# Reordering the first 17 microseconds of a one-core kernel: split x load, earlier weights, transposes in halves, fewer identity matmuls

## The chip, the cores and the metric

The kernel runs on one core of a Trainium2 chip. The metric is the device time of one execution in microseconds (us), lower is better; times are medians of several executions. A change counts as faster or slower only beyond 2%.

Names: PE is TensorE, DVE is VectorE, ACT is ScalarE, POOL is GpSimd, SP is SyncE, which only issues loads here.

## The reference, cut to what matters

```
x = A_x                                    # 1 x 2048 x 1024, bf16
xn = layernorm(x)
out = x + ssm(xn, Lambda, B, C, log_dt, Dskip) + mish(xn @ w1 + b1) @ w2
# ssm: complex diagonal recurrence over 2048 steps, state 1024
# w1: 1024 x 3584, w2: 3584 x 1024
```

Nothing can be multiplied before `x` is normalised and transposed. The first product is `xn @ w1`.

## The kernel before: the parts that matter

The sequence is cut in four blocks of 512 rows, and a block in four x tiles (q = 0 to 3) of 128 rows. Each engine has one queue and works through it in the order written (for ScalarE the profile after the change shows it: two copies with their input ready run only after a mean that waited for its load until 8.85 us); semaphores come from the declared reads and writes. The head, up to the first weight matmuls, is this:

```python
# loads on the SP queue: four x tiles of 256 KB, then weights of 512 KB each
for q in range(NQ):
    load_x(SP, 0, q)
...
for i in range(NRING):
    ring_load()                       # weights for two f tiles
    if i == 3: ...                    # load Dskip

def first_mean_a(q):                  # ACT: sum of a tile, then -sum/D
    aop(activation(sq, xx[q], Identity, accum_out=rc(q, 3)))
    aop(activation(mv[q, 0], rc(q, 3), Copy, scale=-1/D))
def first_var_a(q): ...               # ACT: squares, summed
def first_sums_v / first_var_v ...    # DVE: the same statistics

keep_busy(76)                         # identity matmuls: nothing but PE work
for q in range(2): DVE statistics of tile q
first_sqrt(0); first_mean_a(2); first_sqrt(1); first_var_a(2); first_sqrt(2)   # ACT
first_apply(0)                        # DVE: xn of tile 0
first_transpose(0)                    # PE: 8 transposes into PSUM
keep_busy(4)
first_apply(1)
first_transpose(1)
keep_busy(4)
first_copy(0, VE)                     # DVE: PSUM -> xnT, 8 k slices
first_copy(1, VE, 0, 4)               # DVE: k 0..3
first_copy(1, AC, 4, NK)              # ACT: k 4..7
first_mean_a(3); first_var_a(3); first_sqrt(3)
first_apply(2); first_apply(3)

for f in range(6):                    # 256-wide matmuls: tiles 0 and 1 ("first halves")
    first_half(f, 0)
    if f == 0: transpose the parameters, copy to par
    if f in (2, 3): transpose tile f, copy it (DVE)
...                                   # then first_half(f, 1): tiles 2 and 3 ("second halves")
```

Later the second block's x tiles are loaded from the POOL queue, in the middle of POOL's work on phase tables. VectorE takes their statistics at 45 to 55 us.

```python
for j in range(NJ):
    phases(j)                         # three POOL operations
    if j == 3:
        for q in range(NQ):
            load_x(PO, 1, q)
```

Of the kernel before, what the change touches and what calls it, by code (L numbers as in the profile page):

```python
# [5 lines left out]
ALU = mybir.AluOpType  # L6
# [3 lines left out]
P = 128  # L10
# [146 lines left out]
def build_kernel(nc, A_x, A_Lambda_re, A_Lambda_im, A_B_re, A_B_im, A_C_re, A_C_im,  # L157
                 A_log_dt, A_Dskip, B_w1, B_b1, B_w2, out):
    bf16, f32, i32 = DT.bfloat16, DT.float32, DT.int32
    S, D = A_x.shape[1], A_x.shape[2]  # L160
# [4 lines left out]
    NQ = TB // P  # L165
    NK = D // P
# [8 lines left out]
    PE = Queue(nc, "pe")  # L175
    VE = Queue(nc, "ve")
    AC = Queue(nc, "ac")
    PO = Queue(nc, "po")
    SP = Queue(nc, "sp")

    def sb(name, shape, dtype):
        return nc.alloc_sbuf_tensor(name, shape, dtype)
# [4 lines left out]
    b_ring = [Buf("ring%d" % i) for i in range(NRING)]  # L187
# [16 lines left out]
    b_xnT = [Buf("xnT%d" % q, parts=[Buf("xnT%d_%d" % (q, h)) for h in range(2)]) for q in range(NQ)]  # L204
# [3 lines left out]
    xx = sb("xx", [P, 2, NQ, D], bf16)  # L208
    b_xx = [[Buf("xx%d_%d" % (i, q), parts=[Buf("xx%d_%d_%d" % (i, q, h)) for h in range(2)])
             for q in range(NQ)] for i in range(2)]  # L210
# [7 lines left out]
    NST = 3 * NJ + NF  # L218
    st = sb("st", [NST, P], bf16)
    b_st = Buf("st")  # L220
    ident = sb("ident", [P, P], bf16)
    b_ident = Buf("ident")
    par = sb("par", [P, NST], f32)
    b_par = Buf("par")
    stats = sb("stats", [P, 2, 2, 6], f32)
    b_stats = [Buf("stats%d" % i) for i in range(2)]
# [21 lines left out]
    ps = nc.alloc_psum_tensor("ps", [P, 8, TB], f32)  # L248
    b_ps = [Buf("ps%d" % i) for i in range(8)]

    def ps16(i):
        return ps[:, i, :].bitcast(bf16)
# [23 lines left out]
    vop, aop, pop = VE.op, AC.op, PO.op  # L276
# [7 lines left out]
    def load_x(queue, blk, q):  # L284
        r0 = blk * TB + q * P
        i = blk % 2
        queue.dma(lambda e: e.dma_start(xx[:, i, q, :], A_x[0, r0:r0 + P, :]),  # L287
                  s_xx[i][q] if blk else s_x0[q], writes=[b_xx[i][q]])

    for q in range(NQ):  # L290
        load_x(SP, 0, q)
    for src, r0, n in ((A_log_dt, 2 * NJ, NJ), (A_Lambda_im, NJ, NJ), (A_Lambda_re, 0, NJ),
                       (B_b1, 3 * NJ, NF)):
        AC.dma(lambda e, src=src, r0=r0, n=n: e.dma_start(
# [8 lines left out]
    def ring_load():  # L303
        i = n_loaded[0]
        if i >= len(items):
            return
        n_loaded[0] += 1
        kind, g = items[i]
        s = i % NRING
        if kind == "w1":  # L310
            dst = ring[:, s, :].rearrange("p (k f) -> p k f", k=NK)
            src = B_w1[:, g * 256:(g + 1) * 256].rearrange("(k p) f -> p k f", p=P)
        else:
            dst = ring[:, s, :].rearrange("p (f d) -> p f d", f=2)
            src = B_w2[g * 256:(g + 1) * 256, :].rearrange("(f p) d -> p f d", p=P)
        SP.dma(lambda e: e.dma_start(dst, src), s_ring[s], writes=[b_ring[s]])

    for i in range(NRING):
        ring_load()
        if i == 3:  # L320
            SP.dma(lambda e: e.dma_start(dsk[:], A_Dskip.partition_broadcast(P)), s_dsk, writes=[b_dsk])


# [12 lines left out]
    def rc(q, n):  # L336
        return rs[:, q, n:n + 1]

    def first_sums_v(q, h):
        s = q % 2  # L340
        vop(lambda e: e.bn_stats(stats[:, s, h, :], xx[:, 0, q, h * 512:(h + 1) * 512]),
            reads=[b_xx[0][q]], writes=[b_stats[s]])

    def first_var_v(q):
        s = q % 2
        vop(lambda e: e.bn_aggr(mv[:, q, :], stats[:, s, :, :]), reads=[b_stats[s]], writes=[b_mv[q]])

    def first_mean_a(q):
        aop(lambda e: e.activation(sq[:], xx[:, 0, q, :], AF.Identity, bias=kon[:, 1:2], accum_out=rc(q, 3)),
            reads=[b_xx[0][q], b_kon], writes=[b_sq, b_rs[q]])  # L350
        aop(lambda e: e.activation(mv[:, q, 0:1], rc(q, 3), AF.Copy, scale=-1.0 / D),
            reads=[b_rs[q]], writes=[b_mv[q]])

    def first_var_a(q):
        aop(lambda e: e.activation(sq[:], xx[:, 0, q, :], AF.Square, bias=mv[:, q, 0:1], accum_out=mv[:, q, 1:2]),
            reads=[b_xx[0][q], b_mv[q]], writes=[b_sq, b_mv[q]])

    def first_sqrt(q):
        scale = 1.0 if q < 2 else 1.0 / D
        aop(lambda e: e.activation(rc(q, 1), mv[:, q, 1:2], AF.Sqrt, scale=scale, bias=kon[:, 2:3]),  # L360
            reads=[b_mv[q], b_kon], writes=[b_rs1[q]])

    def first_apply(q):
        y = rc(q, 1)
        vop(lambda e: e.reciprocal(y, y), reads=[b_rs1[q]], writes=[b_rs1[q]])
        vop(lambda e: e.tensor_scalar(xn[:, q, :], xx[:, 0, q, :], mv[:, q, 0:1], y,
                                      op0=ALU.subtract if q < 2 else ALU.add, op1=ALU.mult),
            reads=[b_xx[0][q], b_mv[q], b_rs1[q]], writes=[b_xn[q]])

    def bank_T(q, k):  # L370
        if q == 1 and k >= NK // 2:
            return 5
        return 6 + q % 2

    def first_transpose(q):
        for k in range(NK):
            bank = bank_T(q, k)
            PE.mm(lambda e, k=k, bank=bank: e.transpose(ps16(bank)[:, k * P:(k + 1) * P],  # L378
                                                        xn[:, q, k * P:(k + 1) * P], ident[:]),
                  reads=[b_xn[q], b_ident], writes=[b_ps[bank]],  # L380
                  first=k == 0 or bank != bank_T(q, k - 1), last=k == NK - 1 or bank != bank_T(q, k + 1))

    def first_copy(q, queue, k0=0, k1=NK):
        dst = xnT[:, k0:k1, q * P:(q + 1) * P]
        bank = bank_T(q, k0)
        srcp = ps16(bank).rearrange("p (k t) -> p k t", k=NK)[:, k0:k1, :]
        b_dst = b_xnT[q] if k1 - k0 == NK else b_xnT[q].parts[k0 // 4]
        if queue is AC:
            aop(lambda e: e.copy(dst, srcp), reads=[b_ps[bank]], writes=[b_dst])  # L389
        else:  # L390
            vop(lambda e: e.tensor_copy(dst, srcp), reads=[b_ps[bank]], writes=[b_dst])
# [62 lines left out]

    def keep_busy(n):
        for i in range(n):
            PE.mm(lambda e: e.matmul(ps[:, 4, 0:P], lhsT=ident[:], rhs=ident[:], start=True, stop=True),  # L457
                  reads=[b_ident], writes=[b_ps[4]], first=i == 0, last=i == n - 1)

    keep_busy(76)  # L460
    aop(lambda e: e.activation(rs[:, :, 3], kon[:, 2:3].to_broadcast([P, NQ]), AF.Sqrt), reads=[b_kon], writes=b_rs)
    for q in range(2):
        first_sums_v(q, 0)
        first_sums_v(q, 1)
        first_var_v(q)
    first_sqrt(0)
    first_mean_a(2)
    first_sqrt(1)
    first_var_a(2)
    first_sqrt(2)  # L470
    first_apply(0)
    first_transpose(0)
    keep_busy(4)
    first_apply(1)
    first_transpose(1)
    keep_busy(4)
    first_copy(0, VE)
    first_copy(1, VE, 0, 4)
    first_copy(1, AC, 4, NK)
    first_mean_a(3)  # L480
    first_var_a(3)
    first_sqrt(3)
    first_apply(2)
    first_apply(3)
    NSPLIT = 6

    def first_half(f, half):
        s, fi = f // 2, f % 2
        wt = ring[:, s, :].rearrange("p (k f) -> p k f", k=NK)
        ts = slice(half * 256, half * 256 + 256)  # L490
        for k in range(NK):
            PE.mm(lambda e, k=k: e.matmul(ps[:, f, ts], lhsT=wt[:, k, fi * P:(fi + 1) * P], rhs=xnT[:, k, ts],  # L492
                                          start=k == 0, stop=k == NK - 1),
                  reads=[b_ring[s]] + b_xnT[2 * half:2 * half + 2], writes=[b_ps[f]],
                  first=half == 0 and k == 0, last=half == 1 and k == NK - 1)

    for f in range(NSPLIT):
        first_half(f, 0)
        if f == 0:
            PE.op(lambda e: e.transpose(ps16(5)[:, 0:NST], st[:, :], ident[0:NST, 0:NST]),  # L500
                  reads=[b_st, b_ident], writes=[b_ps[5]])
            vop(lambda e: e.tensor_copy(par[:, :], ps16(5)[:, 0:NST]), reads=[b_ps[5]], writes=[b_par])
        if f in (2, 3):
            q = f
            first_transpose(q)
            first_copy(q, VE)

# [345 lines left out]
```

## Time and profile before

| | before |
|---|---|
| median | 624.05 us (623.83 to 624.13, 3 executions) |
| span of the profiled execution | 622.6 us |
| PE busy | 99% of it |
| first weight matmul | 10.40 us |
| second halves start | 16.77 us |

"Second halves start" is the start of the 49th of the 96 matmuls of 256 columns; from there on PE runs without a wait for 70 us, so this is the time at which the head is over. The page of the kernel before gives the span and, per engine, busy us, share and instructions:

```profile
span 622.6 us, 7430 instructions
...
PE 617.8 (99%) x2981; PEld 289.3 (46%) x2981; DVE 464.5 (75%) x684; ACT 246.7 (40%) x162; POOL 50.2 (8%) x47
```

The waits view of PE, the whole span (who waited for whom: us in total, times, longest):

```profile
PE ps L457 <- POOL kon L328: 1.4, 1, 1.4
PE ps L492 <- ACT xnT L389: 0.5, 1, 0.5
PE ps L715 <- DVE mt L663: 0.3, 1, 0.3
```

PE waits once at the start, once for ScalarE's half copy, and once near 93.7 us for VectorE. As far as waits go, only what PE does before 10.4 us is left to gain on it. The timeline of the head (start, duration, engine, line, operation, out<-in, shape, count, idle time before):

```profile
1.41 7.11 PE L457 MATMUL ps<-ident 128*128 128x128 bf16 x76 [1.41 <-POOL kon L328]
...
6.91 0.55 DVE L366 TENSOR_SCALAR xn<-xx,mv,rs 128x1024 bf16<-128x1024 bf16 x1
...
8.36 0.61 PE L378 MATMUL ps<-ident,xn 128*128 128x128 bf16 x8
...
9.68 0.59 ACT L389 COPY xnT<-ps 128x512 bf16<-128x512 bf16 x1 [0.78 <-PE ps L378]
...
10.16 1.15 ACT L349 ACTIVATE sq<-xx,kon 128x1024 bf16<-128x1024 bf16 x1
...
10.40 1.03 PE L492 MATMUL ps<-xnT,ring 128*128 128x256 bf16 x8 [0.54 <-ACT xnT L389]
```

Read it downward: xn of tile 0 is ready at 7.46 us (6.91 + 0.55), but the identity matmuls (L457) hold PE until 8.36 us, when the transposes (L378) start. ScalarE's half copy (L389) ends at 10.27 us and the weight matmuls (L492) follow. The mean of tile 3 (L349) stands behind that copy. The identity matmuls compute nothing that is used; in this trace the step from one to the next falls from 107 to 56 ns at 7.04 us, and "the clock rises" means this step below.

### The profile page before, as it was taken

How to read it: one execution, taken by the hardware profiler on the slowest of the kernel's cores; microseconds unless marked ns; L12 is line 12 of the kernel's file. 1: busy time of each engine (PE TensorE's matmuls, PEld its weight loads, DVE VectorE, ACT ScalarE, POOL GpSimd, SP SyncE). 2: the span in 40 equal slices, each digit the busy share in tenths (PEclk: the TensorE clock that was granted, in tenths of full speed). 3: DMA queues.
4: the chain of work that ended last, by engine and by line, in shares of the span. 5: the costliest groups of instructions: out<-in, count | busy, mean ns of one | idle time of the engine just before them, and what ended most of it. 6: DMA issues, size and time to landing. Idle time of an engine off the chain costs nothing.

```text
span 622.6 us, 7430 instructions
## 1 busy us (share of the span) xinstructions
PE 617.8 (99%) x2981; PEld 289.3 (46%) x2981; DVE 464.5 (75%) x684; ACT 246.7 (40%) x162; POOL 50.2 (8%) x47
## 2 busy tenths in 40 slices
PE   8999999999999999999999999999999999999998
PEld 8644444444444444444444444444444444444443
DVE  4799999999557599998047759999624856999603
ACT  6679996332069950000008992000000999000000
POOL 1899000000100000000010000000000000000000
DMA  9999976750364400864055420285204541033001
GB/s 265 230 274 272 221 142 187 192 164 1 123 188 161 136 0 18 228 172 125 17 186 148 157 103 0 76 222 158 87 34 136 156 149 68 0 126 111 1 0 68
DMA packets 124188, 79.41 MB, mean 128 GB/s; under 512 B 48890, under 2 KB 106490, under 8 KB 124154
## 3 DMA queue, kind: packets, MB, share of 16 engines
q1 hardware_dynamic: 120656, 71.58, 42.2%
q10 hardware_dynamic: 2538, 4.21, 1.8%
q0 software_dynamic: 960, 3.15, 1.6%
q8 instruction: 24, 0.39, 0.3%
q14 instruction: 10, 0.08, 0.0%
HBM read 63.19 MB, written 4.19 MB: 108 GB/s over the span
## 4 chain that ended last, share of the span: by engine, by line
PE 99%; DVE 0%; ACT 0%; POOL 0%; issue 0%; POOLq 0%
PE ps L715 48%; PE ps L638 29%; PE ps L658 18%; PE ps L492 2%; PE ps L457 1%; DVE mt L663 0%; PE ps L378 0%; DVE xx L752 0%; ACT xnT L389 0%; POOL ident L325 0%; POOL ident L324 0%; PE ps L500 0%; POOL kon L328 0%; POOLq L838 0%
## 5 line engine op out<-in xcount | busy, mean ns | idle before, releaser
L715 PE MATMUL ps<-ring,act 128*128 128x512 bf16 x896 | 194.2, 379 | 0.3 <-DVE mt L663 0.3
L638 PE MATMUL ps<-xnT,ring 128*128 128x512 bf16 x848 | 183.7, 379 | 0.0
L616 ACT ACTIVATE act<-hb 128x3584 bf16<-128x3584 bf16 x16 | 50.9, 3183 | 245.5 <-DVE hb L645 245.0
L715 PEld LDWEIGHTS ps<-ring,act 128*128 128x128 bf16 x896 | 87.6, 98 | 106.3 <-DVE mt L663 0.8
L638 PEld LDWEIGHTS ps<-xnT,ring 128*128 128x128 bf16 x848 | 83.0, 98 | 99.8
L645 DVE TENSOR_SCALAR hb<-ps,par 128x512 bf16<-128x512 f32 x112 | 82.9, 748 | 56.2 <-PE ps L638 54.3
L715 PE MATMUL ps<-CT,hT 128*128 128x512 bf16 x512 | 111.2, 379 | 0.0
L658 PE MATMUL ps<-xnT,BT 128*128 128x512 bf16 x512 | 111.2, 379 | 0.0
L663 DVE TENSOR_TENSOR mt<-ps,tab 128x1024 bf16<-128x1024 f32 x64 | 75.4, 1220 | 13.3 <-PE ps L658 11.7
L715 PEld LDWEIGHTS ps<-CT,hT 128*128 128x128 bf16 x512 | 50.1, 98 | 60.4
L658 PEld LDWEIGHTS ps<-xnT,BT 128*128 128x128 bf16 x512 | 50.1, 98 | 60.4
L752 DVE TENSOR_TENSOR xx<-ps,xx 128x1024 bf16<-128x1024 f32 (+1 forms) x17 | 19.5, 1161 | 70.1 <-PE ps L715 70.0
L681 DVE TENSOR_TENSOR_SCAN hT<-cs,qi,hT 128x512 bf16<-128x512 f32 x48 | 58.9, 1270 | 0.0
L618 ACT ACTIVATE act<-act 128x3584 bf16<-128x3584 bf16 x16 | 51.0, 3191 | 0.2
L617 ACT ACTIVATE act<-act 128x3584 bf16<-128x3584 bf16 x16 | 51.0, 3190 | 0.2
L686 DVE TENSOR_TENSOR mt<-hT,tab 128x1024 bf16<-128x1024 bf16 x64 | 41.4, 689 | 1.1
L623 DVE TENSOR_TENSOR act<-act,hb 128x3584 bf16<-128x3584 bf16 x16 | 32.9, 2059 | 1.3 <-ACT act L618 1.3
L287 POOL DMA_DIRECT2D xx<-in_A_x_dram x12 | 6.7, 558 | 254.0 <-DVE xx L752 250.1
L592 ACT ACTIVATE ct<-CT,cs 128x512 f32<-128x512 bf16 x16 | 11.5, 718 | 28.8 <-DVE CT L594 24.5
L617 ACT ACT_TABLE_LOAD x16 | 20.5, 1283 | 0.3
L618 ACT ACT_TABLE_LOAD x16 | 20.5, 1283 | 0.3
L681 DVE TENSOR_TENSOR_SCAN hT<-cs,hT 128x512 bf16<-128x512 f32 x16 | 18.7, 1209 | 0.0
(78 smaller groups left out, 280.4 us busy)
## 6 DMA issues: line engine op xcount, KB each, us to landing
ring<-in_B_w_dram SPq DMA_DIRECT2D x112, 512.0 KB, 3.7
out_dram<-xx ACTq DMA_DIRECT2D x15, 256.0 KB, 2.0
xx<-in_A_x_dram POOLq DMA_DIRECT2D x12, 256.0 KB, 4.2
xx<-in_A_x_dram SPq DMA_DIRECT2D x4, 256.0 KB, 3.5
dsk<-in_A_Dskip_dram SPq DMA_DIRECT2D x1, 256.0 KB, 6.3
out_dram<-xx ACTq DMA_DIRECT2D x2, 128.0 KB, 1.7
xnT<-xn SPq DMA_TRANSPOSE x12, 4.5
BT<-in_A_B_re_dram SPq DMA_TRANSPOSE x8, 5.7
```

Of the source, the lines that this page charges most:

```text
L616: aop(lambda e: e.activation(a, hs, AF.Exp), reads=[b_hb[g % 2]], writes=[b_act[g]])
L617: aop(lambda e: e.activation(a, a, AF.Ln, bias=1.0), reads=[b_act[g]], writes=[b_act[g]])
L618: aop(lambda e: e.activation(a, a, AF.Tanh), reads=[b_act[g]], writes=[b_act[g]])
L623: vop(lambda e: e.tensor_tensor(a, a, hs, op=ALU.mult), reads=[b_act[g], b_hb[g % 2]], writes=[b_act[g]])
L638: PE.mm(lambda e, k=k: e.matmul(ps[:, bank, :], lhsT=wt[:, k, fi * P:(fi + 1) * P], rhs=xnT[:, k, :], start=k == 0, stop=k == NK - 1), rea ...
L645: vop(lambda e: e.tensor_scalar(hb[:, hs, :], ps[:, bank, :], b1(f), None, op0=ALU.add), reads=[b_ps[bank], b_par], writes=[b_hbf[hs]])
L658: PE.mm(lambda e, j=j, ci=ci, k=k, bank=bank: e.matmul(ps[:, bank + ci, :], lhsT=BT[:, ci, j, k, :], rhs=xnT[:, k, :], start=k == 0, stop= ...
L663: vop(lambda e, s=s, u=u, j=j: e.tensor_tensor(mt[:, s, :, :], u, tab[:, s, j, :].unsqueeze(1).to_broadcast([P, 2, TB]), op=ALU.mult), rea ...
L681: vop(lambda e, ci=ci, init=init: e.tensor_tensor_scan(out=hT[:, ci, j, :], data0=cj("r", j).to_broadcast([P, TB]), data1=hT[:, ci, j, :], ...
L686: vop(lambda e, s=s: e.tensor_tensor(mt[:, s, :, :], hT[:, :, j, :], tab[:, s, j, :].unsqueeze(1).to_broadcast([P, 2, TB]), op=ALU.mult), ...
L715: PE.mm(lambda e: e.matmul(ps[:, u, :], lhsT=lhsT, rhs=rhs, start=st_, stop=last), reads=reads, writes=[b_ps[u]], first=st_, last=last)
L752: vop(lambda e: e.tensor_tensor(xr, src, xr, op=ALU.add), reads=b_src + [b_x], writes=[b_x])
```

## The change

Its intent: start the weight matmuls earlier. The first x tile comes in two loads so that statistics start sooner; the first weights are loaded ahead of tiles 2 and 3; 50 instead of 76 identity matmuls; the transposes of tiles 0 and 1 go to halves of four PSUM banks, so that VectorE and ScalarE copy halves side by side; the parameters' transpose moves out of the matmul stream; tile 2's statistics move from ScalarE to VectorE. Two smaller moves come along: tile 3's transposes stand one f later among the first halves, and the load of Dskip two ring loads later. The diff, cut to its core:

```diff
-    for q in range(NQ):
-        load_x(SP, 0, q)
+    for h in range(2):
+        SP.dma(... xx[:, 0, 0, h*512:(h+1)*512] ...)      # tile 0 in two loads
+    load_x(SP, 0, 1)
@@
     for i in range(NRING):
         ring_load()
-        if i == 3:
+        if i == 0:
+            load_x(SP, 0, 2)
+            load_x(SP, 0, 3)
+        if i == 5:
@@
-        if q == 1 and k >= NK // 2:
-            return 5
+        if q < 2 and k >= NK // 2:
+            return 4 + q
@@
-    keep_busy(76)
+    keep_busy(50)
+    PE.op(... transpose of the parameters into bank 2 ...)
     for q in range(2):
         first_sums_v(q, 0); first_sums_v(q, 1); first_var_v(q)
-    first_sqrt(0)
-    first_mean_a(2)
-    first_sqrt(1)
-    first_var_a(2)
-    first_sqrt(2)
+        first_sqrt(q)
     first_apply(0)
     first_transpose(0)
     keep_busy(4)
     first_apply(1)
     first_transpose(1)
-    keep_busy(4)
-    first_copy(0, VE)
+    first_copy(0, VE, 0, 4)
     first_copy(1, VE, 0, 4)
+    first_mean_a(3)
+    first_copy(0, AC, 4, NK)
     first_copy(1, AC, 4, NK)
-    first_mean_a(3)
     first_var_a(3)
     first_sqrt(3)
+    vop(... copy the parameters to par ...)
+    first_sums_v(2, 0); first_sums_v(2, 1)
+    first_var_v(2)
+    first_sqrt(2)
     first_apply(2)
     first_apply(3)
@@ in the loop over the first halves
-        if f == 0: (transpose and copy of the parameters)
-        if f in (2, 3):
+        if f in (2, 4):
```

The first matmuls (k 0 to 3) now wait only for VectorE's halves, and those with k 4 to 7 only for ScalarE's.

## The prediction

> **What bounds the kernel now.** TensorE: the page has it busy 99% of 622.6 us, and the chain of waits is 99% PE. After 10.4 us the waits view gives it one wait of 0.3 us (near 93.7 us), so only the head can give time. In the timeline the weight matmuls start at 10.40 us and their second halves at about 16.77 us (48 at a 0.109 us pitch before 22.01 us). VectorE has no idle time over 0.15 us from 29.3 to 94 us, but its earlier waits are for PE: a shift of the head moves VectorE too and should reach the end.
>
> **The head before.** 76 identity matmuls run 1.41-8.36 us, at 107 ns each until 7.04 us and 56 ns after. xn of tile 0 is ready at 7.46 us, so they hold the transposes up by 0.9 us. A tile's transposes take 0.45 us, the VectorE copy 0.69 us (0.42 for a half), the ScalarE half copy 0.59 us; that copy (9.68-10.27) releases the matmuls. First weights land at 8.75 us, the fourth x tile at 6.95 us.
>
> **What the change gives.** Half loads start the statistics 0.35 us earlier; xn of tile 0 comes at about 7.1 us. Fifty identity matmuls end at about 6.75 us, so the transposes start at about 7.15 instead of 8.36 us and those of tile 1 end at about 8.5 us. The parameters' transpose leaves the matmul stream (0.2 us). Weights land at about 7 us. VectorE's half copies end at about 8.8 us; four matmuls start.
>
> **What it costs.** ScalarE works in order, and the mean of the fourth tile now stands ahead of both ScalarE half copies, while its load is now behind the first weights. The Trainium skill ("DMA: Bandwidth & Descriptors", HWDGE ordering) says each engine consumes descriptors in ring order; the landings agree (x at 3.6, 4.2, 5.8, 7.0, then weights at 8.75 us). The fourth tile now waits as weights did: it lands at about 8.7 us, estimated from that 8.75. A mean took 1.51 us before (to the next operation), so the half copies run at about 10.2-11.3 us, and matmuls of k from 4 up wait until about 11.45 us, against 10.84 before. After the square pass and two square roots (13.0 us) tile 2's apply follows; its transposes start near 13.9 us, 0.2 us late. Second halves start at about 17.4 us: 0.6 us later. The transposes' gain becomes a ScalarE wait.
>
> **Predicted time:** 624.5 us; 623.1 to 625.5 should hold it 8 times in 10. Chances: faster by over 2% 0.005, within 2% 0.985, slower by over 2% 0.01.
>
> **What would show it.** Right: tile 3's mean starts at 8.4-8.9 us, PE idles 2 us after four matmuls until ScalarE's copy near 11.3 us; second halves start at 17.2-17.6 us. Wrong: the fourth tile lands by 7.5 us, copies end by 9.5, second halves start by 16.2 us.
>
> **What would make it wrong.** (1) The landing: most engines had delivered the first weights by 7.8 us, few late ones held them to 8.75; a landing by 8.0 us makes it a tie or a gain, to about 623. (2) The clock: the skill ("TensorE: Matmul & The Clock Gate", Part 1) says the array runs at half rate until a busy, free-running window of about 3.4 us; this trace steps at 7.04 us. Ending at 6.75 us, then idling, could delay or undo it: up to 1.5 us more.

## The result, and the profile after

Ratios are the mean time of one kernel's executions over that of the other's from the same rounds, so not quite the ratio of the medians quoted. Later runs were made on more than one chip, each beside the kernel before on the same chip, which then stood between 623.51 and 623.79 us.

| | before | after |
|---|---|---|
| median | 623.79 us (623.13 to 624.13, 6 executions) | 624.62 us (623.64 to 626.76, 6 executions) |
| ratio | | 1.0018, 95% interval 0.9999 to 1.0037 |
| first weight matmul | 10.40 us | 9.01 us |
| fifth weight matmul | 10.84 us | 11.34 us |
| second halves start | 16.77 us | 18.67 us (in a half-clock execution) |

The six executions after fall in two groups. Three have a mean granted TensorE clock of 1.000 and took 623.64, 623.79 and 623.89 us: a tie. Three have 0.997 and took 625.34, 625.45 and 626.76 us (the "slow executions" below). One stretch of 3.41 us at half clock gives just this mean (1 - 0.5 * 3.41 / 624 = 0.997). Only one of the three was profiled, the 625.45. Its timeline, with the lines that answer to those above (the same code has moved by a few lines: L457 is now L462, L366 L371, L378 L383, L389 L394, L349 L354, L492 L500):

```profile
1.42 4.33 PE L462 MATMUL ps<-ident 128*128 128x128 bf16 x50 [1.42 <-POOL kon L333]
...
6.74 0.55 DVE L371 TENSOR_SCALAR xn<-xx,mv,rs 128x1024 bf16<-128x1024 bf16 x1
...
7.34 0.62 PE L383 MATMUL ps<-ident,xn 128*128 128x128 bf16 x8 [1.47 <-DVE xn L371]
...
8.44 0.42 DVE L396 COPY xnT<-ps 128x512 bf16<-128x512 bf16 x1 [0.17 <-PE ps L383]
...
8.85 1.15 ACT L354 ACTIVATE sq<-xx,kon 128x1024 bf16<-128x1024 bf16 x1 [1.84 <-DMA xx<-in_A_x_dram]
...
9.01 0.60 PE L500 MATMUL ps<-xnT,ring 128*128 128x256 bf16 x4 [0.39 <-DVE par L486]
...
10.23 1.05 ACT L394 COPY xnT<-ps 128x512 bf16<-128x512 bf16 x2
...
11.34 3.91 PE L500 MATMUL ps<-xnT,ring 128*128 128x256 bf16 x20 [1.73 <-ACT xnT L394]
```

The transposes did move, from 8.36 to 7.34 us, and four weight matmuls start at 9.01 us. Then PE stands for 1.73 us. ScalarE had nothing to do from 7.0 us on, but the next thing in its queue was the mean of tile 3, and that tile landed at 8.82 us. Only after it come the two half copies. The chain of waits of this execution, in order of time (start, us, what), names the same path:

```profile
3.30 5.52 DMA xx<-in_A_x_dram
8.82 0.02 issue
8.85 1.25 ACT sq L354 x2
...
10.32 0.97 ACT xnT L394 x2
...
11.34 3.91 PE ps L500 x20
```

A load that PE needs only for tile 3's transposes (14.58 us in the kernel before, 17.28 us here) now heads the chain. The waits view of PE after:

```profile
PE ps L500 <- ACT xnT L394: 1.7, 1, 1.7
PE ps L383 <- DVE xn L371: 1.5, 1, 1.5
PE ps L462 <- POOL kon L333: 1.4, 1, 1.4
PE ps L500 <- DVE par L486: 0.4, 1, 0.4
```

The 1.5 us wait for L371 is the time from the end of the 50 identity matmuls and the parameters' transpose to xn of tile 0; in the kernel before, the 76 filled it. The 0.4 us put down to the parameters' copy (L486) is for VectorE's half copy: the matmuls do not read `par`, and they start 0.15 us after that half copy ends (8.44 + 0.42 = 8.86 us). Two more things are new beside the long wait for ScalarE. The wait for VectorE near 94 us (0.3 us before) is gone. And the 20 matmuls from 11.34 us take 3.91 us, where 16 took 1.92 us before (timeline at 11.50 us). Their granted clock is in the table by window; the windows follow each other in steps of 3.41 us from the rise of the clock at 4.31 us (window, length, then busy us and instructions of PE, PEld, DVE, ACT and POOL, granted clock, DMA share, GB/s):

```profile
4.31:7.73 3.42, 1.95 (x33) 1.75 (x32) 3.13 (x9) 0.59 (x2) 0.00 (x0) 1.00 1.09 320
7.73:11.14 3.41, 1.50 (x21) 1.04 (x17) 2.58 (x7) 2.26 (x5) 0.00 (x0) 1.00 1.15 309
11.14:14.55 3.41, 3.21 (x16) 2.28 (x17) 1.33 (x4) 3.25 (x7) 0.00 (x0) 0.50 1.20 290
```

From 11.14 to 14.55 us the clock is half (0.50). The window before it has PE busy for 1.50 us of 3.41. In that half-clock window a start-to-start step is 0.213 us, against 0.109 us. The first 16 matmuls from 11.34 us need 15 such steps and took 3.18 us; at 0.109 us they would have taken 1.64 us. That is 1.54 us, and the two groups of executions lie 1.5 to 3 us apart.

### The profile page after: what moved, and what is told of

Same layout as the page of the kernel before. It is cut to its first block, busy times and chain, and to the rows that moved or that the text cites. A ratio compares the mean times of both kernels' runs of the same rounds, so it can differ in the third digit from the quotient of the medians. Undisturbed runs are those within 1.5% of the kernel's fastest.

```text
span 624.0 us, 7314 instructions
## 1 busy us (share of the span) xinstructions
PE 613.6 (98%) x2895; PEld 287.0 (46%) x2951; DVE 465.4 (75%) x687; ACT 244.5 (39%) x158; POOL 49.9 (8%) x47
## 4 chain that ended last, share of the span: by engine, by line
PE 94%; ACT 2%; DVE 1%; DMA 1%; issue 1%; SPq 0%; DVEq 0%
PE ps L719 48%; PE ps L642 26%; PE ps L662 18%; PE ps L500 2%; DMA xx<-in_A_x_dram 1%; ACT act L622 1%; ACT act L621 1%; ACT act L620 1%; DVE hb L649 0%; DVE act L627 0%; ACT L621 0%; ACT sq L354 0%; SPq L287 0%; ACT xnT L394 0%; PE ps L383 0%
```

## The experiments

My theory: the early mean of tile 3, together with the later landing of that tile, blocks ScalarE's half copies; the PE wait that follows eats what the earlier transposes gave, and in some executions costs the full clock as well. Rivals: the copies or the matmuls are held by something else (weights, banks); the slow executions come from late loads; or the end of the head does not matter, since VectorE sets the pace up to 94 us.

All runs below gave the correct result and had a clock of 1.000 in every execution.

### copies_first: the mean behind the copies

```diff
-    first_mean_a(3)
     first_copy(0, AC, 4, NK)
     first_copy(1, AC, 4, NK)
+    first_mean_a(3)
     first_var_a(3)
```

> The changed kernel, with the mean of the fourth x tile moved behind both ScalarE half copies. Theory (the mean, waiting for a late tile, blocks the copies): the copies end near 9.3 us instead of 11.28, PE's fifth weight matmul starts near 9.4 instead of 11.34 us, and the 1.7 us wait for ScalarE's copy is gone. But the square roots of tiles 3 and 2 still come late (12.5 us), so tile 2's transposes start near 13.3 us, with a new PE wait of about 1.6 us for VectorE's apply in front of them, and the second halves start near 16.8 us (before: 16.77). Time 623.0 to 624.0 us. Rival (the copies were held up by something else, or the matmuls wait for the first weights): the fifth matmul stays after 10.5 us.

Measured: 623.31 us (623.13 to 623.77, 5 executions), before 623.74 us, ratio 0.9993 (0.9981 to 1.0005). The fifth matmul starts at 9.26 us and the second halves at 16.66 us. PE's waits, whole span:

```profile
PE ps L383 <- DVE xn L371: 2.0, 2, 1.5
PE ps L462 <- POOL kon L333: 1.4, 1, 1.4
PE ps L500 <- DVE par L486: 0.4, 1, 0.4
```

The wait for ScalarE is gone, as expected, and the fifth matmul comes 2.1 us earlier. The second halves, as expected too, are only about where they were before the change: the wait has moved to tile 2's apply (1.5 of the 2.0 us), because tile 2's square root stands behind tile 3's whole variance on ScalarE. So the order on ScalarE holds PE up at two places.

### both_moved: tile 2's square root ahead of tile 3's squares as well

```diff
     first_copy(0, AC, 4, NK)
     first_copy(1, AC, 4, NK)
     first_mean_a(3)
-    first_var_a(3)
-    first_sqrt(3)
     vop(... par ...)
     (statistics of tile 2 on DVE)
     first_sqrt(2)
+    first_var_a(3)
+    first_sqrt(3)
```

> As copies_first, and the statistics of tile 2 with its square root moved ahead of the square pass of tile 3. Theory: with no ScalarE work in front of what PE waits for, tile 2's transposes start near 11.8 us, and the second halves near 15.2 us, about 1.5 us ahead of the kernel before. If a head start reaches the end whole, the time is about 622.2 us; if VectorE's long stretch without idle time (to 94 us) sets the pace there, part of it is lost and a PE wait for VectorE near 94 us grows by that part: 622.4 to 623.3 us.

Measured: 623.71 us, spread from 622.20 to 625.30 us over 6 executions, all at full clock; ratio 0.9998 (0.9983 to 1.0014). The head is what was expected: fifth matmul at 9.21 us, second halves at 15.09 us, 1.7 us ahead of the kernel before. Two executions (622.20 and 622.21) show that gain at the end; the others lost it. The profiled one took 625.30 us. A line of its VectorE timeline, and the times from issue to landing of its four loads from POOL (view of tile xx at 36 to 38.5 us):

```profile
49.76 1.42 DVE L405 BATCH_NORM_STATS2 stats<-xx 128x6 f32<-128x512 bf16 x2 [3.37 <-DMA xx<-in_A_x_dram]
...
DMA to landing us min/median/max: 7.4/13.0/13.2
```

and two lines of PE's waits:

```profile
PE ps L662 <- DVE hb L649: 1.8, 1, 1.8
...
PE ps L719 <- DVE mt L667: 1.2, 1, 1.2
```

VectorE stood 3.37 us for an x tile of the second block. The four loads issued from POOL at 36 to 38 us landed 7.4 to 13.2 us later (median 13.0), the last near 51 us. VectorE fell behind, and PE twice waited for it. The kernel before showed no such wait in its trace. VectorE gets to those tiles later there (45.12 against 43.45 us for the first), but the larger difference is the landing: its second tile was issued at 38.15 us and landed at 43.52 us, while here it was issued at 36.79 us and landed at 49.73 us. My expectation named VectorE as a possible brake but not the load behind it.

### x_first: the old order of loads, ScalarE as changed

```diff
+    for q in range(1, NQ): load_x(SP, 0, q)     # was: tile 1 alone
     for i in range(NRING):
         ring_load()
-        if i == 0: load_x(SP, 0, 2); load_x(SP, 0, 3)
```

> The changed kernel, with the loads in the order of the kernel before (all x tiles, then weights), ScalarE's order left as changed. Theory (the late fourth tile is what makes the mean block the copies): the fourth tile lands near 7.0 us instead of 8.82, the copies end near 9.6 us, first weights land near 8.8 us, the fifth matmul starts near 9.7 us, second halves near 15.8 us; time 622.5 to 623.5 us. Rival (first weights ahead of x are what allows the early start, so undoing it costs): the first matmul slips well behind 9.0 us and the time is over 624 us.

Measured: 622.80 us, spread from 621.90 to 625.11 us over 6 executions; ratio 0.9989 (0.9974 to 1.0004). Tile 3 lands at 6.16 us instead of 8.82, and the long wait for ScalarE is gone although the mean still stands in front. Here the matmuls wait 1.2 us for the first weights, which in this execution landed at 9.68 us; the fifth starts at 10.17 and the second halves at 15.94 us. (The rival was right that the first matmul slips, to 9.72 us, but not that the time does.) The spread has the same cause as above (VectorE waits 2.8 us for a second-block tile near 49 us in the profiled execution). So either half of the pair cures the wait: tile 3 early, or its mean later. The change made the first late and the second early.

### after_fill: keep PE busy in the wait

```diff
     first_apply(1)
     first_transpose(1)
+    keep_busy(30)
```

> The changed kernel, with 30 identity matmuls (1.7 us at full clock) added behind the transposes of tile 1, inside the wait for ScalarE's copies. Theory (the slow executions of the changed kernel are those in which an idle PE lost the full clock for one 3.4 us window): the fifth matmul still starts near 11.35 us, no execution shows a mean clock under 1.000, all lie within 623.4 to 624.3 us, and none above 625 us. Rival (the slow executions come from loads that land late): executions over 625 us remain, at a full clock.

Measured: 623.78 us (623.64 to 623.94, 5 executions), before 623.74 us, ratio 1.0000 (0.9987 to 1.0013). No execution lost the clock and none is slow. Its timeline at the same place:

```profile
8.34 1.15 ACT L354 ACTIVATE sq<-xx,kon 128x1024 bf16<-128x1024 bf16 x1 [1.51 <-DMA xx<-in_A_x_dram]
...
10.83 1.38 PE L501 MATMUL ps<-xnT,ring 128*128 128x256 bf16 x11 [0.25 <-ACT xnT L394]
```

The wait for ScalarE is as it was, only filled: the fifth matmul starts at 10.83 us, 0.5 us earlier than expected since tile 3 landed 0.5 us earlier here (8.31 us). About 1.5 us of the slow executions is the lost clock, and it is lost because of the wait: three of the six executions of the changed kernel lost it, none of these five did, and none of the 42 executions (these five among them) of all runs built on the changed kernel, in which this wait is filled or gone. (Three of six against none of five alone could be chance.) Without the loss the changed kernel ties with the kernel before: its fifth matmul (10.83 against 10.84 us) and its second halves (16.86 against 16.77 us) are where they were.

### both_x1_pool and both_x1_sp: the second block's x tiles earlier

```diff
 both_x1_pool, on top of both_moved
-        if j == 3:
+        if j == 0:
             for q in range(NQ): load_x(PO, 1, q)
 both_x1_sp, on top of both_moved
-        if j == 3:
-            for q in range(NQ): load_x(PO, 1, q)
+    for q in range(NQ): load_x(SP, 1, q)        # behind the first weights and Dskip, own semaphores
```

> As both_moved, and the loads of the second block's x tiles are issued by GpSimd after its first phase table instead of its fourth, about 15 us earlier. Theory (both_moved has its head start of 1.6 us, and in the slow executions VectorE then stands for a second-block x tile that lands as late as 50 us): no VectorE wait for an x tile is left between 40 and 55 us, the 3.4 us gap near 49.8 us is gone, and all executions lie at 622.0 to 622.6 us. Rival (VectorE's stretch without idle time swallows the head start whatever the loads do): the times stay spread around 623.7 us, with a PE wait for VectorE near 94 us of over 1 us.

> As both_moved, with the second block's x loads issued from the SyncE queue behind the first loads, none from GpSimd. Theory as for both_x1_pool: they land before 30 us, no VectorE wait for x remains, all executions at 621.8 to 622.6 us; GpSimd's tables come 2.3 us earlier, so VectorE collides with GpSimd at other places, worth a few tenths either way. Rival: weights for tile pairs 7 and later land late and PE waits for them between 22 and 40 us; time over 623 us.

Measured: both_x1_pool 622.19 us (622.03 to 622.31, 5 executions), ratio 0.9977 (0.9964 to 0.9989); both_x1_sp 621.96 us (621.82 to 622.50, 5 executions), ratio 0.9974 (0.9962 to 0.9987); before 623.67 us. Second halves start at 15.41 and 15.17 us. The same VectorE operation as above, now in both_x1_pool:

```profile
46.02 1.41 DVE L405 BATCH_NORM_STATS2 stats<-xx 128x6 f32<-128x512 bf16 x2
```

There is no idle time in front of it, the loads landed 3.5 to 6.4 us after issue, and PE has no wait after the head in either trace. The head start reaches the end. Both intervals lie wholly below 1.

### before_x1_sp: the control

The same move of the second block's loads, in the kernel before and nothing else.

> The kernel before with only the second block's x loads moved to the SyncE queue behind the first loads. Control for both_x1_sp: in the kernel before VectorE did not wait for these tiles, so the theory expects no gain from this alone: 623.3 to 624.1 us, ratio 0.999 to 1.0005. If it alone gives 1 us or more, the gain of both_x1_sp is not the head's.

Measured: 623.90 us (623.27 to 623.95, 5 executions), before 623.67 us, ratio 1.0001 (0.9988 to 1.0013). The move alone shows no gain; it only lets a faster head through.

### before_late: does a delay of the head reach the end?

```diff
-    keep_busy(76)
+    keep_busy(96)
```

> The kernel before with 96 instead of 76 identity matmuls, which at full clock delays the first transposes, and with them the weight matmuls and the second halves, by 1.1 us (second halves near 17.9 us). It asks how much of a delay of the head reaches the end. If all of it: 624.85 us, with a PE wait for VectorE near 94 us as before (0.3 us). If the wait near 94 us swallows what it can: 624.3 to 624.5 us, and that wait is gone.

Measured: 624.52 us (624.21 to 625.07, 5 executions), before 623.67 us, ratio 1.0014 (1.0000 to 1.0028). In the profiled execution the clock rose at 5.8 us instead of 7.0, so the delay was smaller than planned: second halves at 17.29 us, 0.52 us after those of the kernel before, and the span is 623.1 against 622.6 us. All of it reached the end, and the wait near 94 us stayed:

```profile
PE ps L715 <- DVE mt L663: 0.3, 1, 0.3
```

So in the kernel before, a delay moves VectorE as well. GpSimd's tables moved along (16.99 us, 0.3 us before the second halves, as in the kernel before). What swallowed part of the delay in the changed kernel is then likely something that the change did to VectorE, or to its timing against GpSimd.

### before_pool_late: only GpSimd's start against the rest

```diff
     turns()
+    pop(tensor_scalar(px[:, 0:256], iot[:, 0:256], cj("thp", 0), ...))   # useless, about 0.9 us
     for j in range(NJ): phases(j)
```

> The kernel before with one useless GpSimd operation of about 0.8 us in front of the phase tables; nothing on PE, VectorE or ScalarE is edited. In every kernel with the changed head, the time from PE's second halves to VectorE's last evacuation of the first block's projection was 73.9 to 74.1 us, against 74.5 us in the kernel before and in before_late. Theory (that 0.5 us is VectorE colliding with GpSimd at other places, as GpSimd's tables start 0.8 us later against the second halves): here too the time shrinks to about 74.0 us, the PE wait for VectorE near 94 us is gone, and the time is 623.2 to 623.4 us. Rival (it comes from VectorE's own changed order in the head): 74.5 us and the 0.3 us wait stay, the time is 623.7 us or more.

Measured: 623.36 us (622.92 to 623.70, 5 executions), before 623.51 us, ratio 0.9995 (0.9982 to 1.0009). GpSimd's timeline, first in the kernel before, then here with the useless operation (L570) in front:

```profile
16.46 1.58 POOL L518 TENSOR_SCALAR px<-iot,cs 128x512 f32<-128x512 f32 x1 [13.55 <-DVE cs L451]
...
15.66 0.94 POOL L570 TENSOR_SCALAR px<-iot,cs 128x256 f32<-128x256 f32 x1 [12.76 <-DVE cs L451]
16.70 1.56 POOL L518 TENSOR_SCALAR px<-iot,cs 128x512 f32<-128x512 f32 x1
```

From the start of the second halves (15.97 us) to the start of VectorE's last pair of evacuations of the first block (90.12 us) is 74.15 us; in the kernel before it is 91.28 - 16.77 = 74.51 us. PE's waits:

```profile
PE ps L457 <- POOL kon L328: 1.4, 1, 1.4
PE ps L492 <- ACT xnT L389: 0.5, 1, 0.5
```

The wait near 94 us is gone, though nothing on PE, VectorE or ScalarE was edited. The clock rose earlier in this execution too, but that is not the reason: in before_x1_sp it also did (second halves at 16.47 us), and there the wait is 0.5 us. The other traces agree: in the three where the tables start 0.3 us before the second halves the stretch is 74.5 to 74.7 us and PE waits near 94 us; in the eight where they start 0.5 to 0.7 us after, and no x tile is late, it is 73.9 to 74.2 us and PE does not wait. So the traces support the theory; the time, 0.15 us by medians, is not clear of noise. How such a collision looks, a line of VectorE's timeline in the kernel before:

```profile
30.45 1.20 DVE L451 TENSOR_SCALAR cs<-cs 128x8 f32<-128x8 f32 x2
```

and the line of GpSimd's timeline at the same time:

```profile
30.25 1.31 POOL L522 TENSOR_TENSOR ph_h<-px,py 128x512 f32<-128x512 f32 x1
```

Two operations of 8 columns, which took 0.38 us at 16.1 us, take 1.20 us here and end at 31.65 us, just after GpSimd's (31.56 us). The Trainium skill ("SBUF — State Buffer", two separate sides) says that VectorE and GpSimd share a pair of ports as "an exclusive lock, not a bandwidth split"; these lines agree. Where such collisions fall depends on when GpSimd's tables start.

### before_50: fewer identity matmuls alone

```diff
-    keep_busy(76)
+    keep_busy(50)
```

> The kernel before with 50 instead of 76 identity matmuls, nothing else. Theory (the identity matmuls held the transposes up): the first transposes start near 7.5 us as xn of tile 0 is ready, the weight matmuls near 9.6 us, the second halves near 15.9 us, 0.9 us ahead of the kernel before: 622.8 us where the second block's x tiles land in time, up to 624.5 us where VectorE stands for one. Rival (the matmuls wait for ScalarE or the weights anyway): second halves at 16.6 us or later, 623.6 us.

Measured: 623.95 us (623.02 to 624.65, 5 executions), before 623.51 us, ratio 1.0002 (0.9990 to 1.0015). In the profiled execution the transposes start at 7.24 us and the second halves at 15.96 us, as expected; then VectorE stands 2.4 us for a second-block tile near 46.8 us, and PE waits 1.2 us for VectorE. Inconclusive as to the part's worth, for a second reason too: in before_pool_late, which has all 76, the second halves started at 15.97 us as well, since the clock rose earlier there and the identity matmuls were over by 7.35 us. The 0.9 us that they cost in the first trace depends on when the clock rises.

### both_xfirst and both_oneload: the two load parts

both_x1_sp with the old order of the first loads, and both_x1_sp with tile 0 in one load.

> both_x1_sp with the first loads in the order of the kernel before (all x tiles, then weights): what the change's load order is worth once ScalarE is not in the way. Theory: first weights land near 9.2 us or later instead of 6.8, the first matmul waits for them (near 9.3 to 9.7 instead of 8.9 us), the second halves come 0.4 to 0.8 us later, time 622.3 to 622.8 us. Rival (x tiles two and three earlier are worth as much): same as both_x1_sp within 0.2 us.

> both_x1_sp with the first x tile in one load again: what the two half loads are worth. In the trace of the changed kernel they start the statistics 0.5 us earlier, but xn of tile 1, on which the copies wait, hangs on the second tile, which landed at 4.8 to 5.0 us. Theory: the half loads are worth nearly nothing, second halves and time within 0.2 us of both_x1_sp (622.0 us). Rival (they carry the head's gain): 0.4 us or more later.

Measured: both_xfirst 621.93 us (621.67 to 622.41, 5 executions), ratio 0.9974 (0.9962 to 0.9987); both_oneload 622.27 us (622.07 to 622.80, 5 executions), ratio 0.9980 (0.9967 to 0.9992); before 623.51 us. For the load order I was wrong: it is worth nothing here. In both_xfirst PE waits 0.5 us for the first weights, which landed at 8.76 us; the first matmul still starts at 8.80 us (8.86 in both_x1_sp), since the transposes came 0.2 us earlier, and the second halves start at 15.08 us. The half loads seem worth about 0.3 us: second halves at 15.46 us with one load against 15.17 with two, and the medians differ by as much. That is more than I expected and less than the rival said, but it is not shown: the intervals overlap, the two runs were made on different chips, and both_x1_pool, with two loads, had its second halves at 15.41 us as well.

## Why the prediction was right or wrong, point by point

The time, 624.5 us predicted against a median of 624.62, agrees better than the reasons do, and that is in part luck. The median lies between two groups, and two terms of the sum were off in opposite directions: the 0.6 us that the head was to cost did not show at full clock (623.8 us), and the lost clock, which was not counted, put half of the executions 1.5 us or more above that.

- **Right: the mechanism.** In one queue an operation that waits for a late load blocks what stands behind it. Predicted: tile 3 lands at about 8.7 us, its mean starts at 8.4 to 8.9 us, the copies run at 10.2 to 11.3 us, the fifth matmul starts at 11.45 us. Measured: 8.82, 8.85, 10.23 to 11.28 and 11.34 us. copies_first (mean moved) and x_first (tile earlier) each take the wait away. But the second halves, predicted at 17.2 to 17.6 us, start at 18.67 us in this half-clock trace and at 16.86 us in after_fill.
- **Right: the landing.** The Trainium skill ("DMA: Bandwidth & Descriptors", queues, rings and completion order) says that each engine consumes descriptors in ring order. Tile 3, now last of the same 1.5 MB, landed when the weights had landed before (8.75 us); in the five other traces with this order it was 8.29 to 8.91 us. The estimate of 8.7 us lies in that range, but a landing 0.4 us earlier undoes most of the predicted loss: in after_fill tile 3 landed at 8.31 us and the second halves start only 0.09 us after those of the kernel before.
- **Half right: what the change gives.** Half loads started the statistics 0.49 us earlier (3.16 against 3.65 us), but xn of tile 0 came at 7.29 us, not 7.1: VectorE finishes tile 1's statistics first, and tile 1 landed at 4.99 us instead of 4.24.
- **Wrong: "a shift of the head moves VectorE too and should reach the end."** The predicted 0.6 us later did not show at full clock: those executions took 623.64 to 623.89 us, a tie. They were not profiled; by after_fill much of the reason is that the head was hardly later at all. The rest is VectorE. In the profiled execution the second halves start 1.90 us later and the span is only 1.4 us longer; 0.3 us of the other 0.5 is the wait near 94 us, which is gone, and 0.2 us was not traced. before_late shows that a delay alone does pass whole. before_pool_late shows in its trace that starting GpSimd's tables later against the matmuls is enough to remove that wait; the changed head starts them 0.5 us after the second halves (19.16 against 18.67 us), the old one 0.3 us before (16.46 against 16.77 us). I had taken VectorE's busy stretch for a fixed length; it was 74.5 us before and 74.0 us after (92.69 - 18.67).
- **Named as a risk, and it happened: the clock.** The prediction gave up to 1.5 us for it and did not count it. Three of six executions lost one window of full clock. The Trainium skill ("TensorE: Matmul & The Clock Gate", Part 1) describes a free-running window of 3413 ns; the trace shows one half-clock window of 3.41 us and 1.54 us lost on the 16 matmuls in it. The reason was off, though: not the early end of the identity matmuls (the clock rose at 4.3 us, while they ran) but the wait for ScalarE. after_fill settles that.
- **Not foreseen:** with a faster head the second block's x loads can land too late for VectorE. That is why both_moved and before_50 gain nothing in the median; both_x1_pool and both_x1_sp show that the loads are the cause.

Open: why loads issued from POOL at 36 us land up to 13 us later. The Trainium skill ("SBUF — State Buffer", two separate sides) warns that GpSimd cannot write descriptors while VectorE holds the shared ports; issued at 20.8 us, before VectorE's long busy stretch, they landed after 3.5 to 6.4 us, which fits, but no run separates this from other traffic. The record shows only a pattern: in the three traces where the first of these loads was issued by 36.91 us (both_moved, before_50, x_first) the slowest of the four took 10.3 to 13.2 us, and in the six where it was issued at 37.04 us or later, 5.0 to 7.8 us. Open too: why one slow execution took 626.76 us, 1.3 us more than the other two.

## What to carry to other kernels

In an in-order queue, put what the bottleneck waits for ahead of anything that waits for a load, and check the landing time of that load after reordering the loads: each move may be harmless and the pair costly. A gain at the head is only kept if every later consumer gets its data earlier as well, so look for loads issued late from a queue that is busy with other work. When PE must wait a microsecond or two, look at the granted clock of the window that follows and at single executions, not only the median.

## What the Trainium skill lacked or had wrong

- "TensorE: Matmul & The Clock Gate": it lets the clock fall after an idle window. Here, in one trace, a window with PE busy for 1.50 us of 3.41 was enough, while one with 1.95 of 3.42 kept the full clock. The page gives no threshold in between.
- "TensorE: Matmul & The Clock Gate": it puts the rise about 4 us into the activity, ±500 ns. Here it came 5.6, 2.9 and 4.4 us after the first matmul (at 7.0, 4.3 and 5.8 us in three traces).
- "SBUF — State Buffer": it names the trap of loads issued from GpSimd beside a busy VectorE, with an example of 3.1 us. Here four loads of 256 KB landed 7.4 to 13.2 us after issue, and 3.5 to 6.4 us after issue when issued 15 us earlier; that this trap is the cause is not shown.
